# A fused attention and token/channel mixer kernel: z^T by two overlapping transposes of the loaded tile, a strided sum, scores held back for the short matmuls, and v asked for earlier

## The chip, the cores and the metric

One core of one Trainium2 chip. The metric is the device time of one launch in microseconds (us). "Before" and "after" are the kernel without and with the change. An interval is a 95% interval. "Span" is the profiled execution on the core; the time told for the launch is about 1.8 us longer.

## The reference

Eight batches of 3008 tokens, cut to what is computed:

```python
# u, v: (8, 3008, 256); z: (8, 3008, 64)
scores = (1 / 3008) * (z @ z^T)
x      = u * (relu(scores) ** 2 @ v)               # gated attention, symmetric scores
h      = relu(x^T @ w_tok1) @ w_tok2               # mixer over tokens, 256 wide
y      = x + h^T
out    = y + relu(y @ w_ch1) @ w_ch2               # mixer over channels, 1536 wide
```

3008 tokens are 23 tiles of 128 and one of 64. Queries are worked in six blocks of 512 (the last 448), keys in six groups of four tiles.

## The kernel before

The program that builds the kernel carries its own scheduler. While it emits instructions it keeps a clock for each engine (`pe`, `free["act"]`, `free["dve"]`, `free["sp"]`), books every operation with a duration written in the source, and picks what TensorE does next by what it believes is ready. The order that comes out is fixed: on the chip each engine runs its list in that order. The last clock, `sp`, is the queue of SyncE, on which all DMA transposes stand one behind the other.

z^T is needed twice, in the lower and the upper 64 partitions, because two score matmuls of 64 rows run side by side on the halves of the array. Before, GpSimd doubles the loaded tile and one transpose of four tiles turns it:

```python
def turn_z(zs, zT, c, engine, tag="zr", bufs=2):
    zr = sb.tile([P, GK, 2, d_qk], BF16, tag=tag, name="zr", bufs=bufs)
    engine.tensor_copy(zr[:], zs.unsqueeze(2).to_broadcast([P, GK, 2, d_qk]))
    nc.sync.dma_start_transpose(
        out=zT[:, c * GK:c * GK + GK, :], in_=zr.rearrange("p t h d -> p (t h d)"))

def on_sp(us):                                     # the queue's clock, before and after
    start = max(free["sp"], pe[0])
    free["sp"] = start + shared(start, us)

def turn_next_z(b, c, zs):
    turn_z(zs, zTs[b + 1], c, nc.gpsimd)
    on_sp(0.6)                                     # booked 0.6 us
    turned[b + 1, c] = Done(pe[0] + 9.0)           # believed ready 9 us later
```

The scores are symmetric, so a diagonal block is made as a triangle and its missing tiles are filled by three small transposes on the same queue, `at<-at` in the profile, called diagonal flips here. Whole blocks below the diagonal come from larger ones, `fl<-at`.

```python
def square_triangle(unit, t):
    ...
    if pr == 0:
        for j, busy in ((0, 0.55), (1, 0.4)):      # booked 0.55 and 0.4 us
            push("sp", t, busy, 5.0, lambda t, j=j: flip_tiles(a3, j))
        return
    ats.pop((b, q, g))
    done = push("sp", t, 0.3, 5.5, lambda t: blocks.update(       # booked 0.3 us
        {(b, q, g): (done, flip_tiles(a3, 2), "at", [1])}))
```

The rest that the change touches: GpSimd puts the columns of the second token weight into tile order after loading (`order_w_tok2`, 13 copies); the sum `x + h` reads PSUM straight; and GpSimd holds the loads of v behind a marker copy of the fifth chunk of the first z.

```python
# in the mixer:  h_ps is in PSUM, xT in SBUF
nc.vector.tensor_add(xT[:, :, :W], xT[:, :, :W], h[:, :, :W])
# at the start
nc.gpsimd.tensor_copy(mark[:, :1], zf0[NG - 2][:, 0, :1])    # NG = 6
for c in range(1, NG):
    load_v(0, c)
# picking TensorE's next work
if n_now and ts <= t + NOW and (whole or (low and n_now >= 2)):
    pick = "scores"
```

The short matmuls of the 64-token tile, called tails here, also run on the halves of the array. Before a group of scores the scheduler does the tails too if it believes them ready, so that one visit to the half-array mode serves both.

## Time and profile before

| | before |
|---|---|
| median of 3 timed runs | 1173.71 us (1171.62 to 1183.31) |
| profiled execution | 1170.49 us, span 1168.6 us, granted clock 0.999 |
| TensorE busy | 99% of the span |
| all 7,049 matmuls at their full-clock rate | 1125.0 us (working in the prediction) |
| visits to half-array mode | 140, 0.202 us each at the median |

How to read it: TensorE is the bound, and only 37.8 us lie between its first and last matmul that are not matmul time. So a change that leaves the matmuls alone can gain little.

### The profile page before, as it was taken

To read this page: it belongs to the slowest core of one execution; us is meant where nothing else is said; L and a number is where in the kernel's file an instruction comes from. 1 tells how busy PE (TensorE), PEld (TensorE's weight loads), DVE (VectorE), ACT (ScalarE), POOL (GpSimd) and SP (SyncE) were. 2 spreads that over 40 slices of the span, in tenths; PEclk is the share of its full clock that TensorE was granted. 3 is DMA by queue.
4 is the path that set the end of the run, shared out by engine and by line. 5 is a ranking of instruction groups with operands and counts; after the bars stand their busy time and mean duration, and the time that the engine had idled before them with its cause. 6 is when DMAs were issued, how large, how long until landed. Compare 5 with 4: busy or idle time off the path is not lost.

```text
span 1168.6 us, 17791 instructions
## 1 busy us (share of the span) xinstructions
PE 1159.7 (99%) x7049; PEld 630.0 (54%) x7049; DVE 541.8 (46%) x819; ACT 521.4 (45%) x650; POOL 158.3 (14%) x328
## 2 busy tenths in 40 slices
PE   9999999999999999999999999999999999999998
PEld 3334554655546555555555655465454655555666
DVE  5785653355333563435634355242552336512544
ACT  7877443244442363343524435344454344513221
POOL 4462001102012100120101210101201000000000
PEclk9999999999999999999999999999999999999999
DMA  9999737997497965896758986798667977632121
GB/s 166 186 157 197 173 92 149 162 190 132 117 167 152 168 132 134 145 181 147 145 131 163 166 152 125 138 186 156 122 141 140 187 145 151 121 100 58 50 82 64
DMA packets 472883, 165.57 MB, mean 142 GB/s; under 512 B 436640, under 2 KB 450528, under 8 KB 472800
## 3 DMA queue, kind: packets, MB, share of 16 engines
q1 hardware_dynamic: 444944, 131.74, 53.6%
q0 software_dynamic: 27344, 32.32, 19.8%
q8 instruction: 55, 0.90, 0.3%
q10 hardware_dynamic: 512, 0.38, 0.1%
q14 instruction: 28, 0.23, 0.1%
HBM read 65.40 MB, written 24.64 MB: 77 GB/s over the span
## 4 chain that ended last, share of the span: by engine, by line
PE 93%; DMA 3%; DVE 2%; POOL 1%; issue 1%; ACT 0%; SPq 0%; ACTq 0%; DVEq 0%; POOLq 0%
PE acc L533 39%; PE op L771 21%; PE hp L729 21%; PE sc L399 6%; PE a_ps L675 4%; PE h_ps L692 3%; DVE at L445 1%; DMA zT<-zr 1%; DMA ur<-in_u_dram 1%; DMA fl<-at 0%; DMA uT<-ur 0%; DMA zf<-in_z_dram 0%; DVE xT L628 0%; ACT at L437 0%; DVE xT L698 0%
## 5 line engine op out<-in xcount | busy, mean ns | idle before, releaser
L742 ACT ACTIVATE h2pre<-hp 128x1024 bf16<-128x1024 f32 (+1 forms) x191 | 191.0, 1006 | 364.5 <-PE hp L729 363.4
L533 PEld LDWEIGHTS <-v_sb 128*128 128x128 bf16 (+1 forms) x2304 | 209.6, 98 | 267.1 <-issue 65.1
L533 PE MATMUL acc<-at,v_sb 128*128 128x512 bf16 (+3 forms) x1464 | 350.7, 378 | 1.9 <-DVE xT L628 1.3
L437 ACT ACTIVATE at<-sc 128x1024 bf16<-128x1024 f32 (+1 forms) x284 | 272.0, 1024 | 159.4 <-PE sc L399 156.1
L445 DVE TENSOR_TENSOR at<-at 128x1024 bf16<-128x1024 bf16 (+1 forms) x284 | 200.7, 716 | 174.3 <-ACT at L437 174.1
L729 PE MATMUL hp<-xT,w_ch_sb 128*128 128x512 bf16 (+1 forms) x1152 | 266.7, 375 | 0.0
L771 PE MATMUL op<-w_ch_sb,h2pre 128*128 128x256 bf16 x2208 | 258.4, 273 | 0.3 <-DVE xT L698 0.2
L771 PEld LDWEIGHTS <-h2pre 128*128 128x128 bf16 x2208 | 215.9, 98 | 46.1 <-issue 0.5
L533 PE MATMUL acc<-fl,v_sb 128*128 128x512 bf16 (+1 forms) x840 | 199.9, 371 | 0.0
L729 PEld LDWEIGHTS <-w_ch_sb 128*128 128x128 bf16 x1152 | 112.7, 98 | 126.8 <-issue 0.2
L784 DVE TENSOR_TENSOR res<-op,u_sb 128x512 f32<-128x512 f32 x87 | 60.1, 691 | 206.5 <-PE op L771 206.5
L744 DVE TENSOR_SCALAR h2pre<-hp 128x1024 bf16<-128x1024 f32 (+1 forms) x97 | 117.3, 1209 | 52.4 <-PE hp L729 51.5
L628 DVE TENSOR_TENSOR xT<-acc,uT 128x512 bf16<-128x512 f32 (+1 forms) x96 | 63.2, 665 | 114.0 <-PE acc L533 113.6
L399 PE MATMUL sc<-zT 64*128 64x512 bf16 (+1 forms) x732 | 95.2, 361 | 0.3
L425 ACT ACTIVATE at<-sc 128x512 bf16<-128x512 f32 (+3 forms) x164 | 59.2, 446 | 67.7 <-PE sc L399 67.5
L125 POOL COPY zr<-zs 128x512 bf16<-128x512 bf16 x42 | 26.1, 623 | 399.6 <-DMA zT<-zr 393.9
L473 DVE TENSOR_TENSOR at<-at 128x512 bf16<-128x512 bf16 (+3 forms) x164 | 44.3, 324 | 59.2 <-ACT at L425 59.2
L399 PEld LDWEIGHTS <-zT 64*128 64x128 bf16 x732 | 31.2, 94 | 56.8 <-issue 39.8
L698 DVE TENSOR_TENSOR xT<-xT,h_ps 128x1024 bf16<-128x1024 bf16 (+1 forms) x48 | 55.6, 1191 | 6.4 <-PE h_ps L692 6.3
L168 POOL DMA_DIRECT2D v_sb<-in_v_dram x48 | 25.9, 545 | 143.7 <-PE acc L533 142.4
L675 PE MATMUL a_ps<-x_sb,w_tok_sb 128*128 128x256 bf16 x384 | 44.7, 273 | 0.0
L692 PE MATMUL h_ps<-w_tok_sb,a_sb 128*128 128x512 bf16 (+1 forms) x192 | 44.5, 374 | 0.1
(43 smaller groups left out, 209.9 us busy)
## 6 DMA issues: line engine op xcount, KB each, us to landing
out_dram<-res SPq DMA_DIRECT2D x87, 256.0 KB, 2.2
v_sb<-in_v_dram POOLq DMA_DIRECT2D x40, 256.0 KB, 4.9
ur<-in_u_dram POOLq DMA_DIRECT2D x40, 256.0 KB, 5.1
zs<-in_z_dram POOLq DMA_DIRECT2D x35, 64.0 KB, 4.4
at<-at SPq DMA_TRANSPOSE x123, 2.4
fl<-at SPq DMA_TRANSPOSE x105, 3.9
v_sb<-in_v_dram POOLq DMA_DIRECT2D x8, 192.0 KB, 6.3
ur<-in_u_dram POOLq DMA_DIRECT2D x8, 192.0 KB, 5.6
```

Of the source, the lines that this page charges most:

```text
L399: nc.tensor.matmul(sc[:, r, c0:c1], zT[h, k * P:(k + 1) * P], zT[h, q * QW + c0:q * QW + c1], start=True, stop=True)
L437: nc.scalar.activation(view, sv, ACT.Relu, scale=inv_S)
L445: nc.vector.tensor_mul(view, view, view)
L533: nc.tensor.matmul(o, vs[blk.b, g][rows, i, dh * P:(dh + 1) * P], rhs, start=first, stop=stop, skip_group_check=True)
L628: nc.vector.tensor_mul(xT[:, dh, :full * P].rearrange("p (t s) -> p t s", s=P), acc[:, :full * P].rearrange("p (t s) -> p t s", s=P), uT[: ...
L675: nc.tensor.matmul(st["a_ps"][:, th, :], w_tok1_sb[:, k, th * P:(th + 1) * P], x[:, :, i, :], start=(k == 0 and th == 0), stop=(k == KT - ...
L692: nc.tensor.matmul(h[:, dh, :W], st["a"][:, th, dh * P:(dh + 1) * P], w_tok2_sb[:, th, q * QW:q * QW + W], start=(th == 0), stop=(th == 1))
L729: nc.tensor.matmul(hp[:, r, :W], w_ch1_sb[:, dc, cc * P:(cc + 1) * P], xT[:, dc, :W], start=(dc == 0), stop=(dc == DT - 1))
L742: nc.scalar.activation(h2[:, :, :W], hp[:, :, :W], ACT.Relu)
L744: nc.vector.tensor_single_scalar(h2[:, :, :W], hp[:, :, :W], 0.0, AX.max)
L771: nc.tensor.matmul(op[:, i, :], h2, w_ch2_sb[:, cc, :], start=(cc == 0 and (i == 0 or apart)), stop=(cc == CHT - 1), skip_group_check=True)
L784: nc.vector.tensor_add(res.rearrange("p i (h d) -> p i h d", d=P), op.rearrange("p i (h d) -> p i h d", d=P), us[:, :, half * 2:half * 2 + ...
```

## The change

Its intent: take work off GpSimd (doubling z, ordering the weight), save visits to the half-array mode, and start the first accumulation earlier. The diff, cut to its core:

```diff
+    zs = consts.tile([P, KT + 2, d_qk], BF16)        # one empty tile at each end
-    def turn_z(zs, zT, c, engine, tag="zr", bufs=2): # ... (shown above)
+    def turn_z(zT, c):
+        for k in (c * GK, c * GK + 1):               # two transposes, one tile apart
+            nc.sync.dma_start_transpose(
+                out=zT[:, k:k + GK:2, :],
+                in_=zs[:, k:k + GK, :].rearrange("p t d -> p (t d)"))
+        if c == LAST:
+            nc.sync.dma_start_transpose(
+                out=zT[:, KT, :], in_=zs[:, KT:, :].rearrange("p t d -> p (t d)"))
...
     def turn_next_z(b, c):
-        turn_z(zs, zTs[b + 1], c, nc.gpsimd)
-        on_sp(0.6)
-        turned[b + 1, c] = Done(pe[0] + 9.0)
+        turn_z(zTs[b + 1], c)
+        on_sp(0.8)
+        for d in [c - 1] * (c > 0) + [c] * (c == LAST):
+            turned[b + 1, d] = Done(pe[0] + 9.0)
...
-            for j, c in enumerate(vorder):           # chunks 0, 5, 1, 2, 3, 4
-                ... ask_z(b, c, h) ... turn_next_z(b, c, h.pop(c))
+                at_group(base + 3 * NG + j, lambda b=b, j=j: load_z(b + 1, j))
+                at_group(base + 3 * NG + j + 3, lambda b=b, j=j: turn_next_z(b, j))
...                                                   # order_w_tok2 goes; the sum:
+                to = xT[:, :, :n * P].rearrange("p h (t s) -> p h t s", t=n)
+                nc.vector.tensor_add(
+                    to, to, h[:, :, :n * P].rearrange("p h (s t) -> p h t s", t=n))
...
-    nc.gpsimd.tensor_copy(mark[:, :1], zf0[NG - 2][:, 0, :1])
+    nc.gpsimd.tensor_copy(mark[:, :1], zf0[NG - 3][:, 0, :1])
...                                                   # late z of batch 0 as "urgent" pieces
+        together = blk is not None and blk.q > 1 and blk.b < B - 1 and (
+            not blk.tails and blk.slot == 0 and tails_ready(blk) > t + 0.3
+            and block_ready(blk, LAST) < FAR
+            or blk.tails and blk.q == NQ - 2 and blk.slot == NG and lead > 3)
-        if n_now and ts <= t + NOW and (whole or (low and n_now >= 2)):
+        if n_now and not together and ts <= t + NOW and (whole or (low and n_now >= 2)):
             pick = "scores"
```

Each batch from 1 to 7 now has 13 z transposes on SyncE's queue in place of six.

More of the change, by code (lines that the diff above doesn't have):

```diff
@@ L45, with __init__ @@
 class Piece:
-    def __init__(self, cost, needs, fn, opens=False, closes=False, room=None):
+    def __init__(self, cost, needs, fn, opens=False, closes=False, room=None,
+                 urgent=False):
         self.cost, self.needs, self.fn = cost, needs, fn
         self.opens, self.closes, self.room = opens, closes, room
+        self.urgent = urgent
 @with_exitstack
@@ L78 @@
     NG = KT // GK
+    LAST = NG - 1
     widths = [min(QW, S - q * QW) for q in range(NQ)]
@@ L110, in load_z @@
     def load_z(b, c):
-        zs = sb.tile([P, GK, d_qk], BF16, tag="zs", name="zs", bufs=6)
         n = full_tiles[c]
-        nc.gpsimd.dma_start(out=zs[:, :n, :], in_=rows_of(z[b], c))
+        k = c * GK + 1
+        nc.gpsimd.dma_start(out=zs[:, k:k + n, :], in_=rows_of(z[b], c))
         if n < GK:
@@ L116, in load_z, with turn_first_z, z_tile @@
                 nc.gpsimd.dma_start(
-                    out=zs[r * TAIL:(r + 1) * TAIL, n, :], in_=last_rows(z[b]))
+                    out=zs[r * TAIL:(r + 1) * TAIL, k + n, :], in_=last_rows(z[b]))
         loading(LOAD / 4)
-        return zs
-    def turn_z(zs, zT, c, engine, tag="zr", bufs=2):
-        zr = sb.tile([P, GK, 2, d_qk], BF16, tag=tag, name="zr", bufs=bufs)
-        engine.tensor_copy(zr[:], zs.unsqueeze(2).to_broadcast([P, GK, 2, d_qk]))
+    def turn_z(zT, c):
[6 more added lines that the diff above has]
+                out=zT[:, KT, :], in_=zs[:, KT:, :].rearrange("p t d -> p (t d)"))
+    def turn_first_z(c):
         nc.sync.dma_start_transpose(
-            out=zT[:, c * GK:c * GK + GK, :], in_=zr.rearrange("p t h d -> p (t h d)"))
+            out=zTs[0][:, c * GK:c * GK + GK, :],
+            in_=double_first_z(c).rearrange("p t h d -> p (t h d)"))
+    def z_tile(b, half, k):
+        return k + 1 - half if b else k
     def first_z(c):
@@ L205, in load_w_tok2 @@
     def load_w_tok2(c):
-        st = sb.tile([P, DT, QW], BF16, tag="h2", name="ws", bufs=ROOM["h2"])
-        W = widths[c]
+        cols = slice(c * QW, c * QW + widths[c])
         nc.gpsimd.dma_start(
-            out=st[:, :, :W],
-            in_=moe_w_tok2.rearrange("(tc t) s -> t tc s", t=P)[:, :, c * QW:c * QW + W])
-        ws[c] = st
-        live["h2"] += 1
+            out=w_tok2_sb[:, :, cols],
+            in_=moe_w_tok2.rearrange("(tc t) s -> t tc s", t=P)[:, :, cols])
         loading(LOAD)
-    def order_w_tok2(c):
-        st = ws.pop(c)
-        live["h2"] -= 1
-        W, n = widths[c], full_tiles[c]
-        for h in range(DT):
-            nc.gpsimd.tensor_copy(
-                w_tok2_sb[:, h, c * QW:c * QW + n * P].rearrange("p (t s) -> p t s", s=P),
-                st[:, h, :n * P].rearrange("p (s t) -> p t s", t=n))
-        if n * P < W:
-            nc.gpsimd.tensor_copy(
-                w_tok2_sb[:, :, c * QW + n * P:c * QW + W], st[:, :, n * P:W])
     def load_w_ch(part):
@@ L237, in load_w_ch @@
         loading(LOAD * 1.5)
-    zTs, vs, urs, uTs, xTs, xs, ws = {}, {}, {}, {}, {}, {}, {}
+    zTs, vs, urs, uTs, xTs, xs = {}, {}, {}, {}, {}, {}
     attn = {}
@@ L251, in flips @@
         return g > q and not direct_block(b, g, q)
-    LAST = NG - 1
     def key_order(b, q):
@@ L396, in score_run @@
             for r, i, c0, c1 in parts(unit):
-                k = g * GK + i
+                k = z_tile(b, r, g * GK + i) * P
+                m = z_tile(b, r, q * GK) * P
                 h = slice(r * d_qk, (r + 1) * d_qk)
                 nc.tensor.matmul(
-                    sc[:, r, c0:c1], zT[h, k * P:(k + 1) * P],
-                    zT[h, q * QW + c0:q * QW + c1], start=True, stop=True)
+                    sc[:, r, c0:c1], zT[h, k:k + P], zT[h, m + c0:m + c1],
+                    start=True, stop=True)
             if pr == 0:
@@ L697, in add @@
                 xT = xTs[b, q]
-                nc.vector.tensor_add(xT[:, :, :W], xT[:, :, :W], h[:, :, :W])
+                n = full_tiles[q]
+                to = xT[:, :, :n * P].rearrange("p h (t s) -> p h t s", t=n)
+                nc.vector.tensor_add(
+                    to, to, h[:, :, :n * P].rearrange("p h (s t) -> p h t s", t=n))
+                if n * P < W:
+                    to = xT[:, :, n * P:W]
+                    nc.vector.tensor_add(to, to, h[:, :, n * P:W])
                 if W < QW and b % 2:
@@ L886, in new_zT @@
     def new_zT(b):
-        zTs[b] = sb.tile([P, KT, P], BF16, tag="zT", name="zT", bufs=2)
+        zTs[b] = sb.tile([P, KT + 1, P], BF16, tag="zT", name="zT", bufs=2)
     vorder = [0, LAST] + list(range(1, LAST))
@@ L895 @@
     load_v(0, 0)
-    nc.gpsimd.tensor_copy(mark[:, :1], zf0[NG - 2][:, 0, :1])
+    nc.gpsimd.memset(zs[:, 0, :], 0.0)
+    nc.gpsimd.memset(zs[:, KT + 1, :], 0.0)
+    nc.gpsimd.tensor_copy(mark[:, :1], zf0[NG - 3][:, 0, :1])
     for c in range(1, NG):
@@ L905, in on_sp, with turn_next_z @@
         free["sp"] = start + shared(start, us)
-    def turn_next_z(b, c, zs):
-        turn_z(zs, zTs[b + 1], c, nc.gpsimd)
-        on_sp(0.6)
-        turned[b + 1, c] = Done(pe[0] + 9.0)
+    def turn_next_z(b, c):
+        turn_z(zTs[b + 1], c)
+        on_sp(0.8)
+        for d in [c - 1] * (c > 0) + [c] * (c == LAST):
+            turned[b + 1, d] = Done(pe[0] + 9.0)
     fetch = {}
@@ L925 @@
         if b + 1 < B:
-            held = {}
-            def ask_z(b, c, held):
-                held[c] = load_z(b + 1, c)
             at_group(base + 3 * NG, lambda b=b: new_zT(b + 1))
             for j, c in enumerate(vorder):
-                at_group(base + 3 * NG + j, lambda b=b, c=c, h=held: ask_z(b, c, h))
-                at_group(base + 3 * NG + j + 3, lambda b=b, c=c, h=held:
-                         turn_next_z(b, c, h.pop(c)))
+                at_group(base + 3 * NG + j, lambda b=b, j=j: load_z(b + 1, j))
+                at_group(base + 3 * NG + j + 3, lambda b=b, j=j: turn_next_z(b, j))
                 if b:
@@ L938, with late_z, turn @@
                              lambda b=b, c=c: load_v(b + 1, c))
-    def turn_late_z(c):
-        zr = double_first_z(c)
-        free["dve"] = max(free["dve"], pe[0]) + 0.45
-        while all(d.t is None for d in ring):
-            run_engines(next_op()[0][0])
-        begin = max(free["dve"] + 0.1, min(d.t for d in ring if d.t is not None))
-        take_slot()
-        begin, end = on_pe(max(pe[0], begin), "full", 0.23)
-        zp = psum.tile([P, GK, P], F32, tag="ps", name="zp", bufs=3)
-        turn_on_pe(zr, zp)
-        turned[0, c] = Done()
-        ring.append(push(
-            "dve", end + 0.1, 0.66, 0.8,
-            lambda t: nc.vector.tensor_copy(zTs[0][:, c * GK:c * GK + GK, :], zp[:]),
-            first=1, done=turned[0, c]))
-    for c in range(GK, NG):
-        at_group(c - GK + 1, lambda c=c: turn_late_z(c))
+    def late_z(c, landed):
+        zr = []
+        def turn(end):
+            take_slot()
+            zp = psum.tile([P, GK, P], F32, tag="ps", name="zp", bufs=3)
+            turn_on_pe(zr[0], zp)
+            turned[0, c] = Done()
+            ring.append(push(
+                "dve", end + 0.2, 0.66, 0.8,
+                lambda t: nc.vector.tensor_copy(zTs[0][:, c * GK:c * GK + GK, :], zp[:]),
+                first=1, done=turned[0, c]))
+        cast = push("dve", landed, 0.42, 0.55, lambda t: zr.append(double_first_z(c)))
+        heads.append(Piece(0.23, [cast], turn, urgent=True))
     at_group(3, lambda: turn_u(0, 0))
@@ L969 @@
     items += [lambda c=c: load_w_tok1(c) for c in range(NG)]
-    first_tok2 = len(items)
     items += [lambda c=c: load_w_tok2(c) for c in range(NG)]
@@ L973 @@
     for k, item in enumerate(items):
-        n = NG + 1 + k * (NQ * NG - 2 * NG + 4) // len(items)
-        at_group(n, item)
-        if 0 <= k - first_tok2 < NG:
-            at_group(n + 4, lambda c=k - first_tok2: order_w_tok2(c))
+        at_group(NG + 1 + k * (NQ * NG - 2 * NG + 4) // len(items), item)
     per_batch = 0.87 * NQ * (2 + CHT // 2) + 1.35 * 4 * NQ
@@ L987 @@
     for c in range(DT, GK):
-        turn_z(zf0[c], zTs[0], c, nc.vector, "h2", 8)
+        turn_first_z(c)
     fill(1)
@@ L994 @@
     score_run(units[:2], 5.3)
+    late_z(4, 7.8)
+    late_z(5, 9.0)
     done_units = 2
@@ L1037 @@
             pick, n_now, ts = "scores", now, t
+        elif tm <= t + NOW and pieces[0].urgent:
+            pick = "mixer"
         elif hold and opened[0] is not None and tm <= t + NOW and pieces is opened[0]:
@@ L1075 @@
         else:
-            budget -= pieces[0].cost
+            if not pieces[0].urgent:
+                budget -= pieces[0].cost
             do_piece(tm, pieces)
```

## The prediction

> **What bounds the kernel now.** I read the page's busy table first, then who waits on TensorE, then the stretches, then the timeline of TensorE alone.
>
> ```profile
> PE 1159.7 (99%) x7049; PEld 630.0 (54%) x7049; DVE 541.8 (46%) x819; ACT 521.4 (45%) x650; POOL 158.3 (14%) x328
> ```
>
> TensorE is busy 99% of 1168.6 us and no other engine reaches half, so only TensorE's own work and the holes in it count. Busy is not peak, so I counted. The timeline and the chain give the rate: 32 hp matmuls of 512 columns take 6.91 us, 0.216 each; 48 op matmuls of 256 take 5.24 us, 0.109 each, which is columns/2400 us + 0.0025. Two 64-row matmuls on the two halves of the array share one such time. All 7,049 matmuls of the built program at that rate (full array 1042.7, half array 82.3) come to 1125.0 us. The change keeps all of them, fillers too: the built program has the same 7,049 with the same shapes. So it can only act on 1168.6 - 1125.0 = 43.6 us: 1.2 before the first matmul, 4.6 from the last matmul's end, 37.8 in between. That alone nearly rules out 2% (23 us).
>
> Where the 37.8 us lie, by the matmuls' start times: first the visits to half-array mode.
>
> ```profile
> 27.33 0.81 PE L399 MATMUL sc<-zT 64*128 64x512 bf16 x6
> 28.07 2.33 PE L533 MATMUL acc<-at,v_sb 128*128 128x512 bf16 x10
> 30.34 0.82 PE L399 MATMUL sc<-zT 64*128 64x512 bf16 x6
> ```
>
> Ten full matmuls should take 2.16 us and the next group starts after 2.27; three half-array pairs should take 0.65 and take 0.74. About 0.10 is lost at each change of mode, on the way in and on the way out. Over the 140 visits of the run the median is 0.202 us a visit: 28 us. Then the start:
>
> ```profile
> POOL mark L897 <- DMA zf<-in_z_dram: 5.3, 1, 5.3
> PE acc L533 <- DVE xT L628: 1.3, 3, 0.7
> PE acc L533 <- DMA v_sb<-in_v_dram: 0.5, 1, 0.5
> ...
> 0.00:26.00 26.00, 23.29 (x117) 8.51 (x118) 14.34 (x26) 18.12 (x20) 8.83 (x21) 1.00 0.95 172
> 126.00:1085.00 959.00, 959.00 (x5838) 526.67 (x5837) 414.33 (x647) 408.30 (x525) 104.55 (x223) 1.00 0.73 143
> ```
>
> In the third column of the last two lines TensorE is busy all of 126 to 1085 us: the start times show no hole there beyond the mode changes. Outside it I find waits of 2.4 us before 6.4 us (first z), 2.1 us from 6.4 to 26 (0.61 and 0.65 around the first late turn, 0.32, 0.48), 2.3 us at block borders from 26 to 126, and 0.8 us at the end.
>
> **What the Trainium skill says.** "TensorEngine Tiling (Array Packing)", Key Properties: changing the tiling mode drains TensorE. The trace agrees, with the 0.20 us a visit. "SBUF — State Buffer", Door 1 (the cacheline note): PSUM has lines of 8 bytes, two fp32 values, and a non-contiguous PSUM pattern slows matmuls down significantly. The new sum reads PSUM at a step of four fp32 values, 16 bytes; but it is VectorE that reads, and "VectorE: DVE Perf Modes", Mode 1x, says that the baseline mode takes odd strides and PSUM operands. The sum is in that mode already:
>
> ```profile
> L698 DVE TENSOR_TENSOR xT<-xT,h_ps 128x1024 bf16<-128x1024 bf16 x40 | 47.3, 1214 | 6.4 <-PE h_ps L692 6.3
> L125 POOL COPY zr<-zs 128x512 bf16<-128x512 bf16 x42 | 26.1, 623 | 399.6 <-DMA zT<-zr 393.9 <-DMA zs<-in_z_dram 5.5
> L126 SPq DMA_TRANSPOSE zT<-zr x44: 1190/1217/2039, 4.4 to 903.1; - x44
> ```
>
> 1214 ns for 1024 elements is about one element a cycle at that page's 0.96 GHz plus a fixed part. No instruction of this trace reads PSUM at a step, so the trace does not decide it. The same SBUF page, Who interferes with whom, has GpSimd's reads contend with VectorE instructions that have two SBUF inputs, as the squares do; I give removing the copies nothing for it, as VectorE is not the bound.
>
> **The change part by part.**
> 1. z^T by overlapping transposes: 42 GpSimd doublings of 623 ns go, 26.1 us of an engine with 86% idle. Value on the path: 0. On the queue of SyncE each chunk now has two transposes of two tiles instead of one of four, and the queue pays nearly by the instruction: 1217 ns for four tiles here, 1.20 us median for those of one to three tiles. So 42 + 7 more at about 1.2 us = 59 us more on that queue in the run. The order shows each batch's transposes ten or more blocks of keys before their first use. Value: 0, risk of some tenths.
> 2. Second token weight in row order: 12 GpSimd copies of 0.5 to 0.8 us and one small one, 9 us, go from batch 0, again off the path. The 48 sums now read PSUM by stride. Chosen: same 1.21 us. Value: 0.
> 3. Scores held back at a block's start so that they go with the short tail matmuls. The built orders count it: half-array visits fall from 140 to 129. Tails alone went from 13 to 2, scores with tails from 30 + 5 to 40 + 6. 11 x 0.202 = -2.2 us, all on TensorE's path.
> 4. First v asked for with z, late turns of z from a ready time. GpSimd's marker copy waited for the fifth z chunk until 7.38 us; now it waits for the fourth, which VectorE was already casting at 4.4. So v leaves GpSimd about 3 us earlier, competing with the last z. I walked the new order of TensorE, ScalarE, VectorE through the start with measured durations (relu 0.94 in this stretch, square 0.69, cast 0.42, copy 0.68, matmul 0.216): the first accumulation of the third key chunk, which stood at 15.76 us behind 16 accumulations, 10 score pairs and two turns, comes at about 14.1 with the same work done. The next block's first accumulation comes at about 23.4 instead of 25.29, a 0.3 us wait for the gate included. -1.9 us, and as TensorE is full afterwards it is kept to the end.
> 5. Waits at later block borders in batch 0 follow from how the squares fall before the gate; the new borders have the same form. 0, give or take 1.
> Sum: -2.2 - 1.9 = -4.1 us, a span of about 1164.5.
>
> **The rivals.**
> A. The strided read of PSUM runs at half rate: 1024 more cycles, about 1.07 us more a sum (an estimate from that page's clock). 42 of 48 sums lie under other work, at some tenths each because they hold one of three PSUM buffers; the six of the last batch lie bare:
> ```profile
> 1092.24 5.52 PE L692 MATMUL h_ps<-w_tok_sb,a_sb 128*128 128x512 bf16 x24
> ...
> 1093.30 6.74 DVE L698 TENSOR_TENSOR xT<-xT,h_ps 128x1024 bf16<-128x1024 bf16 x6 [0.46 <-PE h_ps L692]
> ```
> Already VectorE takes longer here than TensorE. Half rate adds some 5 us here and up to 12 elsewhere: 1172 to 1186 us. For it: the cacheline note. Against: one element a cycle leaves room. 15%.
> B. SyncE's queue becomes the wait: the extra 1.2 us transposes push the flips of the attention tiles behind them, and TensorE waits for fl. For it: flips are issued on that queue and land 3.9 us later. Against: they wait for their data rather than the queue for them, and TensorE shows no wait for fl after batch 0. A few tenths a batch, 1170 to 1174 us. 10%.
> C. Earlier v delays the last two z chunks by sharing the DMA engines, and the start gains nothing: 1171.5 us. The DMA engines were full between 5 and 8 us, which speaks for it; the new order needs the fifth chunk only at about 8 us. 20%.
>
> **Range and chances.** Before: 1171.6, 1173.7, 1183.3 and 1170.5 for the profiled run. 1173.7 - 4.1 = 1169.6; one of the runs is an outlier upward and the median sits a little high, so I say 1169.0. Low 1165: the whole gain and a run like the fastest. High 1175: gain lost to C, or part of A. Faster by 2% would need half of all the idle time there is: 0.01. Slower by 2%, 1197 us, needs more than A gives: 0.03.
>
> **What would show it.** Half visits at 129 with 0.20 us each; the first accumulation of the second block near 23.4 us; the wait for v gone; sums still near 1.21 us (A wrong) or above 2 us (A right); about twice the transposes for z^T, each still near 1.2 us, and no wait of TensorE for them or for fl. I am wrong if the start is not earlier, if holes appear between 126 and 1085 us, or if the sum's duration moves.

## More of the kernel before

The prediction shows the page's busy line, the waits and the stretches. One more line belongs beside them, the page's chain of work that ended last, by engine:

```profile
PE 93%; DMA 3%; DVE 2%; POOL 1%; issue 1%; ACT 0%; SPq 0%; ACTq 0%; DVEq 0%; POOLq 0%
```

SyncE's queue (SPq) has no share in it.

The queue around the last query block of batch 2, one line for each run of like entries (start us, us, engine, line, operation, count):

```profile
332.69 2.52 SPq L126 DMA_TRANSPOSE zT<-zr  x2
335.31 1.26 SPq L640 DMA_TRANSPOSE x_sb<-xT  x1
336.66 2.69 SPq L126 DMA_TRANSPOSE zT<-zr  x2
339.44 3.86 SPq L485 DMA_TRANSPOSE at<-at  x3
```

Four z transposes in 332 to 339 us, then the three diagonal flips. Each entry holds the queue for 1.26 to 1.35 us.

## The result, and the profile after

| | before | after |
|---|---|---|
| median, same rounds | 1176.51 us (1171.62 to 1183.31, 4 runs) | 1219.17 us (1204.78 to 1221.25, 4 runs) |
| ratio | | 1.0332 [1.0234, 1.0430] |
| profiled span, granted clock | 1168.6 us, 0.999 | 1203.0 us, 0.988 |

Ratios here and below are the mean time of one kernel's runs over the mean of the other's of the same rounds, so not quite the ratio of the medians. The profiled execution of after, 1204.78 us, was the fastest of its four, so the account below is of the mildest case.

The page's busy line and chain of after:

```profile
PE 1162.9 (97%) x6955; PEld 632.8 (53%) x7049; DVE 549.8 (46%) x839; ACT 512.0 (43%) x638; POOL 128.1 (11%) x275
...
PE 87%; SPq 5%; DMA 4%; issue 2%; DVE 1%; ACT 0%; POOL 0%; ACTq 0%; DVEq 0%; POOLq 0%
```

TensorE's busy time rose by only 3 us (94 of its 7,049 matmul records are missing from this trace), so most of the time lies in holes; and SyncE's queue, absent from the chain before, has 5% of it. Who TensorE waited for (us in total, times, longest us):

```profile
PE acc L534 <- DMA at<-at: 12.8, 3, 4.6
PE acc L534 <- issue: 6.7, 17, 4.2
PE sc L400 <- DMA zT<-zs: 5.6, 2, 5.2
PE sc L400 <- DMA zT<-zr: 4.3, 2, 2.9
```

and the two stretches that the prediction showed of before:

```profile
0.00:26.00 26.00, 20.35 (x96) 7.29 (x99) 12.41 (x22) 14.80 (x16) 10.86 (x27) 0.93 1.00 180
126.00:1085.00 959.00, 930.89 (x5561) 510.07 (x5636) 421.78 (x658) 390.05 (x506) 86.24 (x185) 0.99 0.74 141
```

From 126 to 1085 us TensorE was busy all 959 us before; now 28 us of it are idle. Of these, 22.2 us are five waits, one near the end of each of five successive batches, at 214, 355, 504, 650 and 794 us. They are of two kinds. In the first, TensorE waits for z^T itself, whose last transposes went out at 214.42 us:

```profile
219.76 1.46 PE L400 MATMUL sc<-zT 64*128 64x512 bf16 x6 [5.25 <-DMA zT<-zs]
```

In the other four it waits for a diagonal flip. Take the one at 355. The queue of SyncE in after:

```profile
343.59 7.64 SPq L129 DMA_TRANSPOSE zT<-zs  x6
351.33 1.26 SPq L641 DMA_TRANSPOSE x_sb<-xT  x1
352.68 2.48 SPq L129 DMA_TRANSPOSE zT<-zs  x2
355.22 1.22 SPq L133 DMA_TRANSPOSE zT<-zs  x1
356.54 3.77 SPq L486 DMA_TRANSPOSE at<-at  x3
```

and beside it VectorE's last squares before these flips, then TensorE (in brackets: idle before, and what ended it):

```profile
348.35 0.43 DVE L474 TENSOR_TENSOR at<-at 128x256 bf16<-128x256 bf16 x2 [5.78 <-ACT at L426]
349.00 1.09 DVE L474 TENSOR_TENSOR at<-at 128x512 bf16<-128x512 bf16 x4 [0.23 <-ACT at L426]
354.14 1.68 PE L534 MATMUL acc<-fl,v_sb 128*128 128x448 bf16 x8
360.40 0.56 PE L534 MATMUL acc<-at,v_sb 64*128 64x448 bf16 x2 [4.58 <-DMA at<-at]
360.73 1.51 PE L400 MATMUL sc<-zT 64*128 64x512 bf16 x6
```

Nine z transposes and one other stand without a gap from 343.59 to 356.44, then the diagonal flips until 360.31. The first flip had its data by 350.1 us at the latest and went out at 356.54: it stood over 6 us in the queue. TensorE, whose order was written in the belief that it had long gone by, stands before the tail matmuls from 355.8 until 360.40. It goes on once that first flip has landed, 3.7 us after it went out (the view of the tile `at` on SyncE, 356.4 to 357.6 us). At 504, 650 and 794 us it is the same: the first flip behind the z transposes goes out at 505.04, 652.15 and 796.14, lands 3.7, 3.1 and 2.4 us later, and TensorE goes on at 508.79, 655.37 and 798.60, each time within 0.2 us of the landing. (The profile puts the last of these waits down to "issue".) There is a second loss in TensorE's last line: six scores that took 0.82 us elsewhere take 1.51. The stretches around it (us, busy time and count of PE, PEld, DVE, ACT, POOL, then granted TensorE clock, DMA share, GB/s):

```profile
350.00:356.00 6.00, 5.82 (x28) 2.55 (x26) 1.47 (x3) 1.02 (x1) 0.00 (x0) 1.00 0.40 87
356.00:360.40 4.40, 0.00 (x0) 0.03 (x1) 0.00 (x0) 0.00 (x0) 0.57 (x1) 0.77 0.61 99
360.40:365.00 4.60, 4.60 (x16) 1.67 (x17) 2.08 (x3) 2.85 (x3) 0.00 (x0) 0.50 0.59 134
365.00:370.00 5.00, 5.00 (x30) 2.03 (x29) 2.08 (x3) 3.66 (x4) 2.13 (x4) 0.98 1.06 166
```

After 4.58 us of idleness the clock is 0.50 for 4.6 us, about 2 us more lost. The Trainium skill, "TensorE: Matmul & The Clock Gate", What's actually happening, says this: half rate after an idle window of about 3.4 us, full rate after about 3.4 us of sustained work. This trace agrees in kind, with half rate after 4.58 us of idleness and 0.98 from 365 us on, and the prediction had left it out.

The start, on GpSimd's row: the marker of after is there 3 us sooner than the 7.38 us of before, as intended.

```profile
4.34 0.27 POOL L907 COPY mark<-zf 128x1 f32<-128x1 f32 x1 [1.99 <-DMA zf<-in_z_dram]
4.55 2.66 POOL L185 DMA_DIRECT2D v_sb<-in_v_dram  x5
```

But the two first z transposes of SyncE land late. The view of the tile z^T over the first 20 us ends, before and then after, with

```profile
DMA to landing us min/median/max: 3.1/3.7/4.3
```

```profile
DMA to landing us min/median/max: 6.8/8.4/10.1
```

and TensorE waits for them:

```profile
11.45 0.61 PE L400 MATMUL sc<-zT 64*128 64x512 bf16 x4 [1.40 <-DMA zT<-zr]
...
16.14 0.39 PE L400 MATMUL sc<-zT 64*128 64x512 bf16 x2 [2.89 <-DMA zT<-zr]
```

The first gate, which closes the first query block, came at 28.72 us instead of 24.54 (VectorE, `xT<-acc`): the start is 4 us later, where the prediction had it 1.9 us sooner.

The account of the 34.4 us between the two spans, from the matmuls' start times against their full-clock durations: the five waits 5.25 (z^T) + 12.8 (three flips) + 4.15 (the one at 794) = 22.2 us; the slow clock behind them some 9.5; the first 25 us lose 10.0 in place of 6.4, so 3.6 more; fewer visits to half-array mode, -2.2. Together 33.1.

The strided sum, by form (busy us, mean ns, idle before it):

```profile
L702 DVE TENSOR_TENSOR xT<-xT,h_ps 128x1024 bf16<-128x1024 bf16 x40 | 47.3, 1216 | 15.3 <-PE h_ps L693 15.2
```

1216 ns where the contiguous one took 1214.

### The profile page after: what moved, and what is told of

It is laid out like the page before. It is cut to its first block, busy times and chain, and to the rows that moved or that the text cites.

```text
span 1203.0 us, 17732 instructions
## 1 busy us (share of the span) xinstructions
PE 1162.9 (97%) x6955; PEld 632.8 (53%) x7049; DVE 549.8 (46%) x839; ACT 512.0 (43%) x638; POOL 128.1 (11%) x275
## 4 chain that ended last, share of the span: by engine, by line
PE 87%; SPq 5%; DMA 4%; issue 2%; DVE 1%; ACT 0%; POOL 0%; ACTq 0%; DVEq 0%; POOLq 0%
PE acc L534 36%; PE op L779 20%; PE hp L737 19%; PE sc L400 6%; PE a_ps L676 3%; SPq L129 3%; PE h_ps L693 3%; DMA at<-at 1%; DMA u_sb<-xT 1%; DMA ur<-in_u_dram 1%; DMA zT<-zs 1%; DVE xT L702 1%; DMA uT<-ur 0%; ACT at L438 0%; SPq L486 0%
## 5 line engine op out<-in xcount | busy, mean ns | idle before, releaser
L534 PE MATMUL acc<-at,v_sb 128*128 128x512 bf16 (+3 forms) x1439 | 349.7, 381 | 19.4 <-DMA at<-at 12.8
L534 PEld LDWEIGHTS <-v_sb 128*128 128x128 bf16 (+1 forms) x2304 | 212.3, 98 | 291.7 <-issue 80.1
L750 ACT ACTIVATE h2pre<-hp 128x1024 bf16<-128x1024 f32 (+1 forms) x179 | 179.9, 1007 | 361.8 <-PE hp L737 355.8
L446 DVE TENSOR_TENSOR at<-at 128x1024 bf16<-128x1024 bf16 (+1 forms) x284 | 194.9, 688 | 221.7 <-ACT at L438 219.5
L534 PE MATMUL acc<-fl,v_sb 128*128 128x512 bf16 (+1 forms) x817 | 196.6, 377 | 1.9 <-issue 0.8
L752 DVE TENSOR_SCALAR h2pre<-hp 128x1024 bf16<-128x1024 f32 (+1 forms) x109 | 130.9, 1201 | 71.0 <-PE hp L737 70.7
L400 PE MATMUL sc<-zT 64*128 64x512 bf16 (+1 forms) x732 | 99.6, 373 | 10.2 <-DMA zT<-zs 5.6
L702 DVE TENSOR_TENSOR xT<-xT,h_ps 128x1024 bf16<-128x1024 bf16 (+1 forms) x48 | 54.3, 1171 | 15.3 <-PE h_ps L693 15.2
L196 POOL DMA_DIRECT2D ur<-in_u_dram x48 | 26.0, 543 | 175.3 <-DMA uT<-ur 168.2
```

What stands on the lines that cost most here:

```text
L400: nc.tensor.matmul(sc[:, r, c0:c1], zT[h, k:k + P], zT[h, m + c0:m + c1], start=True, stop=True)
L446: nc.vector.tensor_mul(view, view, view)
L534: nc.tensor.matmul(o, vs[blk.b, g][rows, i, dh * P:(dh + 1) * P], rhs, start=first, stop=stop, skip_group_check=True)
L702: nc.vector.tensor_add(to, to, h[:, :, :n * P].rearrange("p h (s t) -> p h t s", t=n))
L750: nc.scalar.activation(h2[:, :, :W], hp[:, :, :W], ACT.Relu)
L752: nc.vector.tensor_single_scalar(h2[:, :, :W], hp[:, :, :W], 0.0, AX.max)
```

## The experiments

**The theories.** T1, the bookings: the order of TensorE is made from wrong durations of SyncE's queue, and the waits come from meeting that queue too early. T2, the count: the queue simply has more entries than it can take. T3, early v: v shares the DMA engines with the first z. T4, holding back: the new rule for scores makes TensorE come to the tails at a bad moment. T5: the strided read. Medians are given as "this / before of the same job".

**1. z^T alone, in the kernel before** (natural order of chunks, as the new scheme needs).

```diff
 # before, plus only:
+        for k in (c * GK, c * GK + 1): nc.sync.dma_start_transpose(... zs[:, k:k + GK, :] ...)
+        on_sp(0.8)
```

> The kernel before with the overlapping z transposes alone (old marker, old late turns, old second token weight, no holding back of scores). Theory Q (the 49 extra transposes on SyncE's in-order queue push the diagonal flips of the attention tiles behind them, and TensorE waits): 1195 to 1215 us, with one wait of 4 to 5 us in five or six batches. Theory T (holding scores back puts the tail matmuls where the diagonal flips are not back yet): no such waits, 1170 to 1176 us.

1204.15 / 1172.40 us, ratio 1.0223 [1.0149, 1.0296]. TensorE waits 13.4 us for the diagonal flips (3 times) and 12.2 for z^T. The z part alone brings most of the loss, with no early v, no hold and no stride. (The profiled run, 1213.39, was the slowest of its four; 7.45 us of its waits, for z^T near 87 us, are not in after's profiles.) It also needs only 133 visits to half-array mode: the fewer visits are not the hold's alone.

**2. All of the change but z^T.**

```diff
 # after, with before's load_z, turn_z, turn_next_z
-        on_sp(0.8)
+        on_sp(0.6)
```

> The changed kernel with the old doubled z and one transpose a chunk, all else changed. Theory Q: the waits in the batches are gone, the slow start stays: 1172 to 1178 us. Theory T: the waits stay, 1195 us or more.

1198.23 / 1172.40, ratio 1.0185 [1.0124, 1.0247]. So the rest is not innocent either: 7.6 us of waits for the first z^T at the start, two waits for diagonal flips, 9.5 us, and one of 3.8 us for ScalarE's relu at 115 us. The expectation's second theory had the time, but the flip waits are two, at 780 and 926 us, and not the five waits of after.

**3. After, with the marker of before.**

```diff
-    nc.gpsimd.tensor_copy(mark[:, :1], zf0[NG - 3][:, 0, :1])
+    nc.gpsimd.tensor_copy(mark[:, :1], zf0[NG - 2][:, 0, :1])
```

> The changed kernel with the marker on the fifth z chunk again, so that v is asked for after z as before. Theory M (the early v shares the DMA engines with the first z transposes, which then land at 11 and 16 us): the two waits of 1.4 and 2.9 us of the start go, and with them the slow clock after them: 5 to 8 us faster than the changed kernel, the batches unchanged (1196 to 1214 us). If the late turns themselves are the cause: the waits stay.

1211.99 / 1172.40, ratio 1.0296 [1.0228, 1.0364]. The start loses 6.5 us again, as before, in place of 10.0. But another wait appears, 8.49 us for z^T near 87 us, so the total hardly moves, and the 5 to 8 us of the expectation are not shown by the ratios (their intervals overlap). Early v is tested alone in experiment 9.

**4. After, with the z transposes booked at what they take.**

```diff
-        on_sp(0.8)
+        on_sp(2.45 if c < LAST else 3.7)
```

> The changed kernel with the scheduler told what the z transposes really cost on SyncE's queue (2.45 us a chunk, 3.7 for the last, in place of 0.8). The instructions are the same, only their order moves. Theory Q: the scheduler puts other work where TensorE waited; the waits shrink to under 1.5 us each: 1172 to 1185 us. If the queue itself is full and no order helps: no better than 1195 us.

1190.09 / 1172.40, ratio 1.0108 [1.0044, 1.0172]. The work is the same (one relu of 288 moves from VectorE to ScalarE), only a number of the scheduler is put right, and against after's 1.0332 some 26 us come back, though not down to the 1172 to 1185 us expected. The waits of TensorE in this trace, of the slowest of the four:

```profile
PE sc L400 <- DMA zT<-zr: 8.0, 2, 6.0
PE sc L400 <- DVE res L792: 6.0, 1, 6.0
PE acc L534 <- DVE xT L629: 4.9, 1, 4.9
...
PE acc L534 <- DMA at<-at: 0.3, 1, 0.3
```

The waits for the flips are gone; the start's remain, and two new ones, each of a single occurrence.

**5. The count alone: before, each z transpose cut into two instructions.**

```diff
-        nc.sync.dma_start_transpose(
-            out=zT[:, c * GK:c * GK + GK, :], in_=zr.rearrange(...))
+        for t in (0, 2):
+            nc.sync.dma_start_transpose(
+                out=zT[:, c * GK + t:c * GK + t + 2, :],
+                in_=zr[:, t:t + 2].rearrange(...))
```

> The kernel before, each chunk's z transpose cut into two instructions of two tiles; the same bytes, the same order on TensorE, VectorE and ScalarE, 44 more entries of about 1.2 us on SyncE's queue. If the length of the queue alone makes the waits (theory Q in its plain form): waits of some us appear in most batches, 1180 us or more. If the new place of TensorE's and SyncE's instructions against each other is what makes them (theory O: the order comes from a scheduler that books 0.3 to 0.6 us for a transpose that takes 1.2, and the order of before happens to leave room): under 1176 us.

1178.50 / 1172.62, ratio 1.0047 [0.9995, 1.0098]. The order on TensorE, ScalarE and VectorE is the same as before's, and the queue holds 12 z transposes a batch, nearly as many as after's 13:

```profile
336.50 5.06 SPq L127 DMA_TRANSPOSE zT<-zr  x4
341.65 1.26 SPq L642 DMA_TRANSPOSE x_sb<-xT  x1
343.00 6.36 SPq L127 DMA_TRANSPOSE zT<-zr  x4
349.45 4.33 SPq L487 DMA_TRANSPOSE at<-at  x3
```

The flips go out 10 us later than in before (349.45 against 339.44; TensorE itself is 3 us behind there), yet TensorE shows no wait for them anywhere: before's order has other work at that place. T2 alone is worth some 5 us, about 0 to 11 by the interval. (Two of the four runs were near 1174 and two near 1184; only a 1173.89 one was profiled, so what the slower two met is open. The kernel before itself ran from 1170 to 1179 in this job.)

**6. The stride alone: before, with the weight in row order and the strided sum.**

```diff
-                nc.vector.tensor_add(xT[:, :, :W], xT[:, :, :W], h[:, :, :W])
+                nc.vector.tensor_add(to, to, h[:, :, :n * P].rearrange("p h (s t) -> p h t s", t=n))
```

> The kernel before with the second token weight in row order and its sum read by stride, nothing else; the order on TensorE is the same. Sum unchanged at 1.21 us, as the profile of the changed kernel has it: the same time as before within 3 us, no new wait.

1170.09 / 1172.62, ratio 0.9994 [0.9945, 1.0043]. T5 falls.

**7. Bookings put right everywhere, marker of before.** This differs from experiment 3 in bookings alone.

```diff
-        on_sp(0.8)
+        on_sp(2.45 if c < LAST else 3.7)
-            for j, busy in ((0, 0.55), (1, 0.4)):
+            for j, busy in ((0, 1.2), (1, 1.2)):
-        done = push("sp", t, 0.3, 5.5, ...
+        done = push("sp", t, 1.2, 5.5, ...
-                free["sp"] = max(free["sp"], t) + 0.4          # output
+                free["sp"] = max(free["sp"], t) + 0.53
```

> The changed kernel with the marker on the fifth z chunk again and the scheduler told 1.2 us for each small transpose (z, diagonal flips) and 0.53 for an output. Theories Q and O: no waits for flips or z transposes in the batches, half-array visits at 134: 1168 to 1176 us, 0 to 5 us from before. If the waits stay in other places, so that the costs of the queue are not the reason: 1185 us or more.

1182.53 / 1172.62, ratio 1.0069 [1.0029, 1.0109]. From 1.0296 to 1.0069 is about 27 us, for numbers in the scheduler; the time is still above the 1168 to 1176 us expected. In the same batch as above, the queue and TensorE of this run:

```profile
335.64 10.21 SPq L129 DMA_TRANSPOSE zT<-zs  x8
345.90 1.22 SPq L133 DMA_TRANSPOSE zT<-zs  x1
...
358.81 2.85 SPq L486 DMA_TRANSPOSE at<-at  x2
```

```profile
354.88 2.78 PE L779 MATMUL op<-w_ch_sb,h2pre 128*128 128x256 bf16 x24
357.50 0.92 PE L534 MATMUL acc<-fl,v_sb 128*128 128x448 bf16 x4
358.36 0.82 PE L400 MATMUL sc<-zT 64*128 64x512 bf16 x6
359.11 0.93 PE L534 MATMUL acc<-fl,v_sb 128*128 128x448 bf16 x4
359.88 2.78 PE L779 MATMUL op<-w_ch_sb,h2pre 128*128 128x256 bf16 x24
```

The queue is as crowded as ever, nine z transposes in a row. The flips come no earlier than in after, now behind other entries (left out at the dots), 12 us after the last z transpose. TensorE does mixer work while they run and has no hole. Two waits of other kinds are left in this execution, the slowest of the four. One is for z^T, 4.3 us. The other, 5.3 us, comes from a single flip `fl<-at` at 571 us that held the queue 7.10 us, where 1.68 is the median in after's trace; the transpose behind it, then the residual, the gate and TensorE came late in turn.

**8. The same late marker and bookings as in experiment 3, z asked for and turned one query block earlier.**

```diff
-            at_group(base + 3 * NG + j, lambda b=b, j=j: load_z(b + 1, j))
-            at_group(base + 3 * NG + j + 3, lambda b=b, j=j: turn_next_z(b, j))
+            at_group(base + 2 * NG + j, lambda b=b, j=j: load_z(b + 1, j))
+            at_group(base + 2 * NG + j + 3, lambda b=b, j=j: turn_next_z(b, j))
```

> The changed kernel with the marker on the fifth z chunk and each batch's z asked for and turned one block of queries (6 key chunks) earlier; the scheduler keeps its small figures. If what matters is that the z transposes stand right before the diagonal flips of the last block: waits gone, 1168 to 1178 us. If the scheduler's figures are what matters, waits come up at another block: 1185 us or more.

1198.21 / 1172.62, ratio 1.0215 [1.0162, 1.0267]. Moving the entries elsewhere gives back some 10 us of 35; the flip waits shrink to 2.2 us, but z^T is waited for in five places, 15.3 us. So moving the entries is no cure. That the wrong bookings make these waits too is argued, not shown: the one flip went out at 692.04 us, before TensorE stopped, and was 12.7 us under way.

**9. Early v alone, in the kernel before.** All orders are the same as before's.

```diff
-    nc.gpsimd.tensor_copy(mark[:, :1], zf0[NG - 2][:, 0, :1])
+    nc.gpsimd.tensor_copy(mark[:, :1], zf0[NG - 3][:, 0, :1])
```

> The kernel before with one figure changed: the marker copy waits for the fourth z chunk instead of the fifth, so v is asked for about 3 us earlier. The order on every engine is the same. Theory M (early v slows the first two z transposes): TensorE waits for those transposes before 20 us, the time rises by 3 to 8 us. If early v only helps: 1 to 2 us faster.

1179.46 / 1170.63, ratio 1.0092 [1.0056, 1.0128]. The landing of the two first z transposes here, from the same view as above, and the wait it makes:

```profile
DMA to landing us min/median/max: 11.9/13.4/14.9
```

```profile
8.08 1.47 PE L533 MATMUL acc<-at,v_sb 128*128 128x512 bf16 x6 [0.21 <-DMA v_sb<-in_v_dram]
16.50 1.04 PE L399 MATMUL sc<-zT 64*128 64x512 bf16 x4 [6.95 <-DMA zT<-zr]
```

So T3 holds: asking for v 3 us earlier delays z^T by about 10 us, and TensorE waits 7 of them. The Trainium skill, "DMA: Bandwidth & Descriptors", Issuing engines are not separate DMA queues, says that transfers of all engines run on the same 16 DMA engines and interleave. The trace agrees: loads issued by GpSimd stretch a SyncE transpose from 3.7 to 13.4 us.

**10. Holding back alone, in the kernel before.**

```diff
+        together = blk is not None and blk.q > 1 and blk.b < B - 1 and (...)
-        if n_now and ts <= t + NOW and (whole or (low and n_now >= 2)):
+        if n_now and not together and ts <= t + NOW and (whole or (low and n_now >= 2)):
```

> The kernel before with the holding back of scores alone: 131 half-array visits in place of 140. By the step of the prediction: 9 x 0.20 = 1.8 us faster. By theory O (any new order may put work of TensorE ahead of transposes that SyncE issues later than booked): one to three waits of about 5 us for diagonal flips, 5 to 20 us slower.

1186.08 / 1170.63, ratio 1.0131 [1.0116, 1.0147]. 131 visits instead of 140, and two waits for diagonal flips, from 763 and 911 us:

```profile
PE acc L532 <- DMA at<-at: 11.8, 2, 6.6
```

The rule itself, on the old z, costs 15 us: it changes which work TensorE has left when the flips are due. But what made the flips late is not what it was in after. Here is the queue, the landing of its first flip (view of the tile `at` on SyncE, 759 to 760.5 us), and TensorE:

```profile
759.31 6.73 SPq L484 DMA_TRANSPOSE at<-at  x4
```

```profile
DMA to landing us min/median/max: 9.3/9.3/9.3
```

```profile
768.66 0.55 PE L532 MATMUL acc<-at,v_sb 64*128 64x448 bf16 x2 [5.18 <-DMA at<-at]
```

This flip went out 4 us before TensorE stopped, and was 9.3 us under way, where 2.4 is the median of the diagonal flips in this trace; the one at 907 us took 10.1. The scheduler believes in 5.0 to 5.5. The DMA engines' share was 1.30 from 759 to 768.6 us. So here the flips were slow to land, not slow to go out; in experiment 2 too, the first flips took 8.4 and 7.9 us. What booking these landings at such times would do was not tried. With experiments 9 and 10, experiment 2 is about their sum: 1.0092 and 1.0131 against 1.0185.

**11. All but z^T, marker of before, true bookings.**

```diff
 # experiment 2, plus: zf0[NG - 2] again, flips booked 1.2, output 0.53, and
-        on_sp(0.6)
+        on_sp(1.22)
```

> All of the change but the overlapping z transposes and the early v, with the scheduler told the real queue times (1.2 us a small transpose, 0.53 an output): 133 half-array visits. If the booking is what makes the waits: no wait over 2 us after the start, 1167 to 1174 us, at best 2 us faster than before. If waits of 4 us or more stay: the booking is not all of it.

1182.35 / 1170.63, ratio 1.0074 [1.0015, 1.0134]; three runs near 1182 to 1186 and one of 1168.84. No wait for diagonal flips is left. The profiled run (1181.93) has one large wait, 9.8 us for ScalarE's relu: at 94.03 us one flip `fl<-at` held the queue 9.43 us, so attention buffers did not come free. The fast run suggests that this one hold is not always there; why a flip is held so long just then is not settled.

**12. The control: before, true bookings.**

```diff
-        on_sp(0.6)                                # and flips 1.2, output 0.53
+        on_sp(1.22)
```

> The kernel before with the scheduler told the real queue times, nothing else: 139 visits. Its order has no waits to lose: the same within 4 us. If it gets slower by more, then the order of before is one that happens to fit, and truer queue times alone don't make a good order.

1172.39 / 1170.63, ratio 1.0017 [0.9995, 1.0040]. Right bookings are no gain by themselves; before's order was already free of these waits, with its wrong ones.

**13. After again**, nothing changed, beside the next two.

> The changed kernel once more. Its profiled execution was 14 us faster than its other three. If its waits come and go from one execution to the next: this profile shows a further wait, most likely for the z transposes near 86 us that two related kernels had (about 8 us with the slow clock after it), in an execution near 1215 us. If every execution has the same waits and the rest is something else: the same five waits in the batches and two at the start, with the time spread evenly.

1212.61 / 1170.72, ratio 1.0360 [1.0314, 1.0405]. The same five waits. The start's wait for z^T was 7.8 us here and 4.3 in the first profile, so a part of the spread among after's executions, 1204.78 to 1221.25, lies there. A 1220 us execution was never profiled, so the rest of the spread is open.

**14. After without holding back.**

```diff
-        together = blk is not None and ...
+        together = False and blk is not None and ...
```

> The changed kernel without the holding back of scores: 132 half-array visits in place of 129. If the z transposes and their booking make the waits: the five waits stay, 1205 to 1220 us. If the holding back, which alone cost 15 us, adds its own share here: 1195 us or less.

1213.40 / 1170.72, ratio 1.0370 [1.0347, 1.0392]: the same as experiment 13. Under the z part's waits the hold costs nothing more, nor does it gain; and there are 132 visits without it.

**15. Experiment 14 with marker of before and true bookings.**

```diff
+        on_sp(2.45 if c < LAST else 3.7)          # flips 1.2, output 0.53
+    nc.gpsimd.tensor_copy(mark[:, :1], zf0[NG - 2][:, 0, :1])
```

> The overlapping z transposes, the row-order weight and the late turns, with true queue times in the scheduler, v asked for as before, and no holding back: 138 visits. The version that the runs so far point to: no wait over 2 us from 125 us on, at most one for z near 86 us: 1168 to 1178 us. Another wait of 5 us in a later batch says that the booking is still not the whole reason.

1169.54 / 1170.72, ratio 1.0002 [0.9974, 1.0030]. From +3.7% to nothing. One of the four runs, the profiled one, took 1175.91, with a wait of 2.9 us for z^T near 86 us, in batch 0; the other three lie at 1168.8 to 1169.8. With the queue's true durations, the late marker and no hold, the overlapping transposes, the strided sum and the urgent pieces cost nothing that four runs show. So the loss falls to three parts: the bookings (experiments 3 and 7, about 27 us), early v, and a remainder that goes with the hold: 1.0069 and 1.0074 in experiments 7 and 11, with it and true bookings, against 1.0002 here without it. That the hold makes the remainder is argued from these three ratios, not shown: the waits in the traces of 7 and 11 are for z^T and behind long flips.

Over all profiled runs the pattern is this. With true bookings of z (experiments 4, 7, 11, 12, 15, 16, 17) TensorE waits at most 0.3 us for diagonal flips. With wrong ones and an order other than before's (after, 1, 2, 3, 8, 10, 13, 14) it waits 2.2 to 13.4 us. With wrong ones and before's order (before, 5, 6, 9) it does not wait. So it is not one lucky order that took these waits away. Waits for z^T are another matter: with true bookings 2.9 to 9.5 us for batch 1's z^T are left in experiments 7, 15 and 16.

**16. Experiment 15, batch 1's z believed ready later**, against that wait.

```diff
-            turned[b + 1, d] = Done(pe[0] + 9.0)
+            turned[b + 1, d] = Done(pe[0] + (15.0 if b == 0 else 9.0))
```

> As e15, and for batch 1 the scheduler books the landing of the z transposes 15 us after they are handed over instead of 9. If the wait at 86 us is again a booking: it goes, in all executions, and the time falls to 1164 to 1169 us, 2 to 5 us under before. If it comes back a few us later: the DMA engines, over 100% booked there, set the pace, and the time is that of e15.

1175.91 / 1171.27, ratio 1.0025 [0.9993, 1.0056]; a miss, the 1164 to 1169 us expected did not come. The profiled run, 1185.74, the slowest, still waits 9.5 us for z^T there.

**17. Experiment 15, batch 1's z asked for three groups earlier.**

```diff
-            at_group(base + 3 * NG + j, ...)
+            z0 = base + 3 * NG - (3 if b == 0 else 0)
+            at_group(z0 + j, ...)
```

> As e15, and the z of batch 1 asked for and turned three key chunks earlier. If room ahead of the first use is all it needs: as e16, 1164 to 1169 us. If the earlier loads only crowd the DMA engines elsewhere in batch 0: a wait of 2 us or more before 90 us, and no gain.

1169.67 / 1171.27, ratio 0.9986 [0.9955, 1.0018]. The middle stretch is full again:

```profile
126.00:1085.00 959.00, 958.94 (x5846) 527.09 (x5846) 427.48 (x662) 398.89 (x512) 82.97 (x185) 1.00 0.75 143
```

This is the best form of the change that I found. It is level with before: the interval holds 1, so no version is shown to beat it, and the gain of 2 to 5 us that was expected is not shown.

## Why the prediction was wrong

It said 1169.0 us (1165 to 1175) and gave "slower" 3 in 100. Measured: 1219.17 us. Point by point, by its own steps:

1. **z^T: "Value: 0, risk of some tenths."** This is the step that failed, and rival B with it. Its counts were right: twice the entries, still near 1.2 us each. It then counted 59 us of extra queue over the run and looked only at when z^T itself is first used, "ten or more blocks of keys" later. It did not ask what stands behind those entries, nor what the scheduler believes of them; and even the first use came too soon once, in the wait of 5.25 us for z^T at 214 us. In place of "a few tenths a batch" there were five waits of 4.0 to 5.3 us, 22.2 us together, and 9.5 us of slow clock. Four of them were for the diagonal flips, where rival B had looked at the whole-block flips, "fl". "They wait for their data rather than the queue for them" does not hold in after: a flip whose data was there by 350.1 us stood behind z transposes until 356.54. The wrong booking was in the diff to be read, 0.8 us for what the prediction's own numbers put at 2.4. What made the waits was shown by undoing it: experiments 3 and 7 differ in bookings alone and by 27 us, while nearly the same count of entries under before's order cost some 5 us, 0 to 11 by the interval, and no wait for a flip (experiment 5).
2. **The strided sum: 0.** Right: 1216 against 1214 ns, and experiment 6 is level. Rival A was wrong.
3. **Holding back: "11 x 0.202 = -2.2 us".** The visits did fall to 129, and a visit still costs 0.202 us. But the step credited the hold with it; 133 visits come with the new z alone, and 132 in after without the hold. And it valued the mode changes only, not the order they imply: alone the hold costs 15 us, in two waits for flips that were 9.3 and 10.1 us under way (experiment 10).
4. **Earlier v: -1.9 us.** The wrong sign: +3.6 us in the profiled after, and +0.9%, about 10 us, alone. Rival C had the mechanism, the shared DMA engines, and expected "the start gains nothing". But it looked at the last z chunks, which arrive from memory; the ones hurt were chunks 2 and 3, already loaded and being turned by a transpose. The walk of the start used landing times of before, which the change itself altered.
5. **Block borders in batch 0: 0, give or take 1.** Not tested by itself; nothing in the account needs it.

What the prediction named as the sign of its being wrong, holes between 126 and 1085 us, is what the profile showed first. Its range was narrow because it took TensorE's freedom from waits in before as a property of the kernel. It was a property of one order.

What stays open: why some `fl<-at` flips hold the queue so long (seven of after's 105 held it over 5 us, up to 11.50; two of before's, up to 5.58), what delayed the z^T of the wait at 214 us (its transposes went out at 214.42 and 215.75 and landed 5.1 and 4.0 us later, against a median of 2.34), and what sets the spread among after's executions beyond the start's wait.

## What to carry to other kernels

A static order is only as good as the durations it was made with: when a change alters the number of entries on a queue, correct the scheduler's booking of that queue in the same change, and look in the trace at what stands behind the new entries rather than at their sum. A TensorE that shows no wait says that its present order avoids them, not that the queues beside it have room. A transfer can also be late after it has gone out: where the DMA engines are full (a share of 1.30 in experiment 10), its landing belongs in the order too. And a wait on TensorE like these, of 4.0 to 5.3 us, should be priced with the slow clock behind it, here some 2 us each.

## What the Trainium skill lacked or had wrong

- "DMA: Bandwidth & Descriptors", DMA Transpose: neither it nor the rest of the page gives a time on the issuing queue for a transpose from SBUF to SBUF of few tiles on this chip. Here one entry took about 1.2 to 1.3 us at the median whether it turned one tile or eight (1.22 for the one-tile z entry, 1.20 for two, 1.29 for u's eight), and 1.68 for sixteen.
- The same page: nothing says that such an entry can hold its queue far longer while the DMA engines are busy; single ones took 7.10, 9.43 and 11.50 us here (experiments 7 and 11, and after), with a DMA share of 1.21 to 1.36 meanwhile; nor that a small one can be 9 to 10 us under way (experiment 10).
- "SBUF — State Buffer", Door 1, the note on PSUM lines: it leaves open whether VectorE's reads suffer. A read at a step of four fp32 values took 1216 ns against 1214 ns contiguous for 1024 elements.
